# Thresholded attention and a gated two-layer block on one core: single-slot scores at the start, an earlier projection, and a new order inside a slot

## The chip, the cores and the metric

The kernel runs on one core of a Trainium2 chip. A time is device microseconds from one launch. Times before and after are medians of several runs; a profile is one more execution, with its own time. The engines are TensorE (PE, with its weight loads shown apart), VectorE (DVE), ScalarE (ACT), GpSimd (POOL) and SyncE (SP), which here only issues DMAs.

## The reference

There are 8 batches of 8 heads, with 576 rows and 64 columns each. What is computed is attention with a threshold, then two matrix products with an activation between them:

```python
scores = scale * np.matmul(q, k.transpose(0, 1, 3, 2))
thresh = np.max(scores, axis=-1, keepdims=True) - tau
scores = np.where(scores >= thresh, scores, -1000000000.0)
scores = scores - np.max(scores, axis=-1, keepdims=True)
attn = np.exp(scores)
attn = attn / (np.sum(attn, axis=-1, keepdims=True) + 1e-09)
attn_out = np.matmul(attn, v)
x = attn_out.transpose(0, 2, 1, 3).reshape(4608, 512)
h = x @ w_in                       # 512 -> 2048
g = h * np.clip(h + 3.0, 0.0, 6.0) / 6.0
out = g @ w_out                    # 2048 -> 512
```

## The kernel before

**Slots.** The work is cut into 144 slots, 18 for each batch. A slot is 128 query rows for two heads (`a` = 0, 1) against all 576 keys. Four heads form a "quad"; their q and k lie in 32-partition groups, so one slot uses two of PE's four row groups and the next slot (`i` = 1) the other two. The tiles run (quad 0: t 0, 1), (quad 1: t 0, 1), the 64 rest rows of both quads (t = 4), (quad 0: t 2, 3), (quad 1: t 2, 3), two slots for each.

**One slot's way.** Scores go from PE to PSUM in float32 (L224). DVE copies them to SBUF and takes the maximum (`sm_max`, L238). POOL makes the bias (L247). ACT masks with a Prelu (L252) and takes the exponential with its sum (L257). DVE inverts the sum (L260), POOL normalises to bf16 (`sm_norm`, L265). The result is transposed by a DMA that SP issues (L276), or, for the slots marked `on_chip`, by nine PE transposes (L282) and a DVE copy (L283). The attention product with v (L290) writes PSUM, and DVE casts it to `xT` (L298). Then the projection (`mm1`, L313 with `w_in_sb`), the activation in two steps (`mm1_relu` on ACT in odd slots and on DVE in even ones, L331 and L333; `mm1_gate` on DVE, L346), and the second projection (`mm2_part`, L313 with `w_out_sb`), whose finished token tile of 128 rows is evicted by DVE (`mm2_out`, L365) and stored.

**PSUM.** One tile holds eight banks. An even slot's scores take bank 2 (448 "own" columns) and 128 columns at the end of bank 1, an odd slot's bank 0 and 128 columns at the head of bank 1; the second head uses banks 3 to 5 in the same way. Products use banks 2 and 5 in turn (`bank()`), which are the own banks of even slots. `HB` = 6 takes the projection and the PE transposes, `OB` = 7 the second projection.

**Order.** The order of the work is written out by hand, slot by slot, in one loop; each engine runs its instructions in that order, and waits come from the data. In slot n the loop gives: the maximum of slot n+1, the inverse of slot n-1, waiting copies (PE transposes and token tiles), one projection item if n is at least `N1` = 15 and one is there, the attention products of slot n, the item's activation, a PE transpose, in odd slots two parts of the second projection, the exponentials of slot n, the masks of slot n+1, transposes of q and k (`jobs`), the normalisation of slot n-1, in even slots the scores of n+2 and n+3 together (`burst`), some filler matmuls (`warm_up`), and DMA issues (`issues`). Inside a burst a no-op on POOL stands between two groups of matmuls that share a bank.

**Items.** A projection item is 256 tokens of one batch by 256 columns of `w_in`: 8 items for each chunk of 256 tokens, and rest items for the 64 rows left of each batch. A chunk's items come free when the last of its four head pairs has had its product: for batch 0 at slots 14 and 24, then every batch at its own slots 14 and 24. Items and parts that are left after slot 143 are done after the loop.

**Loads.** SP loads q (four DMAs) and k (one) per quad into two alternating buffers; the first k goes by ACT's queue. DVE transposes them in 32x32 blocks (L104, L118). POOL loads v and the two weights, with a cast.

Of the kernel before, what the change touches and what calls it, by code (L numbers as in the profile page):

```python
# [15 lines left out]
P = 128  # L16
# [4 lines left out]
def kernel(  # L21
# [10 lines left out]
    nc = tc.nc  # L32
# [4 lines left out]
    KI = d_model // P  # L37
    NI = d_ff // P
    NSLOT = 18
    N1 = 15  # L40
    HB, OB = 6, 7
    R, T = 32, S // 32
    scale = 1.0 / math.sqrt(D)
# [24 lines left out]
    qkT = {}  # L68
# [7 lines left out]
    def at(when, n, job):  # L76
        when.setdefault(n, []).append(job)
# [4 lines left out]
    def load(quad, of, t0=0, t1=T, by=nc.sync):  # L82
        b, g = divmod(quad, 2)
        if quad not in nat:
            nat[quad] = (nat_pool.tile([P, T * D], F32, tag="nq", name="nq"),
                         nat_pool.tile([P, T * D], F32, tag="nk", name="nk"))
        dst = nat[quad][of][:, t0 * D:t1 * D]
        if of:
            src = k[b, 4 * g:4 * g + 4].rearrange("h (r t) d -> (h r) (t d)", r=R)
            by.dma_start(out=dst, in_=src[:, t0 * D:t1 * D])  # L90
            return
        for c in range(4):
            by.dma_start(out=dst[32 * c:32 * c + 32].rearrange("p (t d) -> p t d", d=D),
                         in_=q[b, 4 * g + c].rearrange("(t r) d -> r t d", r=R)[:, t0:t1])
# [7 lines left out]
    def transpose_q(quad, t0, t1):  # L102
        rows = nat[quad][0][:].rearrange("p (t j w) -> p t j w", j=2, w=32)
        nc.vector.transpose(out=qk_of(quad)[0][:].rearrange("p j (t w) -> p t j w", w=32)[:, t0:t1],  # L104
                            in_=rows[:, t0:t1])
# [3 lines left out]
    def transpose_k(quad, part):  # L109
        first, e = ((0, 5), (10, 4))[part]  # L110
        rows = nat[quad][1][:].rearrange("p (t j w) -> p j t w", j=2, w=32)
        outs = qk_of(quad)[1]
        for j in range(2):
            for_u = rows[:, j, first:first + 2 * e].rearrange("p (u e) w -> p u e w", u=2)
            base = outs[:, j, :]
            o = base[:, 64 * part:64 * part + 64].rearrange("p (u w) -> p u w", u=2)
            o = bass.AP(tensor=o.tensor, offset=o.offset, ap=[list(o.ap[0]), [32, 2], [128, e], [1, 32]])
            nc.vector.transpose(out=o, in_=for_u)  # L118
# [31 lines left out]
    load(0, 1, 0, 10, by=nc.scalar)  # L150
    load(0, 0, 0, 4)
    load(0, 1, 10, T, by=nc.scalar)
    load(0, 0, 4, T)
    load(1, 1)
    load(1, 0)

    identf = singles.tile([P, P], F32)
# [20 lines left out]
    def bank():  # L178
        nonlocal turn
        turn += 1  # L180
        return ps[:, (2, 5)[turn % 2], :]
# [7 lines left out]
    for b in range(B):  # L189
        for g, t in ((0, 0), (0, 1), (1, 0), (1, 1), (None, 4), (0, 2), (0, 3), (1, 2), (1, 3)):  # L190
            for i in range(2):
                sl = Slot()
                sl.b, sl.g, sl.t, sl.i, sl.n = b, g, t, i, len(queue)
                sl.on_chip = sl.n in (1, 3, 5, 7, 8, 9, 11)
                queue.append(sl)


# [3 lines left out]
    def score_col(n, a):  # L201
        return (512 - OWN if n % 2 else 1024 - P) + 1536 * a

    def behind(one, other):
        tc.add_manual_dep(one.ins, other.ins.name, mybir.DependencyInfo(
            mybir.DependencyClass.Sync, mybir.DependencyReason.DATA), reason="bank")

    def burst(n):
        steps = ((0, 0, P, 0), (1, 0, OWN, 0), (0, 0, P, 1), None,
                 (0, P, OWN, 0), (1, 0, OWN, 1), (0, P, OWN, 1), (1, OWN, P, 0), (1, OWN, P, 1))  # L210
        for step in steps:
            if step is None:
                relay = nc.gpsimd.nop()
                behind(relay, mm)
                continue
            i, k0, w, j = step
            sl = queue[n + i]
            for a in range(2):
                c = 32 * (2 * i + a)
                c0 = score_col(n + i, a) + k0  # L220
                for quad, rows, q0 in (((2 * sl.b + sl.g, slice(0, P), sl.t * P),) if sl.t < 4 else
                                       [(2 * sl.b + g, slice(64 * g, 64 * g + 64), 512) for g in range(2)]):
                    qT, kT = qkT[quad]
                    mm = nc.tensor.matmul(ps_flat[rows, c0:c0 + w],  # L224
                                          qT[c:c + 32, j, q0:q0 + rows.stop - rows.start],
                                          kT[c:c + 32, j, k0:k0 + w], start=(j == 0), stop=(j == 1))
                    if (i, k0) == (1, OWN):
                        behind(mm, relay)

    def sm_max(sl):  # L230
        sl.s = s_pool.tile([P, 2, S], F32, tag="s", name="s")
# [61 lines left out]
    def av_main(b, hp, chunk):  # L293
        if hp == chunk == 0:
            xT[b] = x_pool.tile([P, KI, 512], BF16, tag="xT", name="xT")
        pb = bank()[:, 0:256]
        av(pb, b, hp, pts[b, hp, chunk], slice(0, 256))
        nc.vector.tensor_copy(out=xT[b][:, hp, 256 * chunk:256 * chunk + 256], in_=pb)  # L298

# [94 lines left out]
    for b in range(B):  # L394
        n0 = b * NSLOT
        for hp in range(NPAIR):
            at(products, n0 + 8 + 2 * hp, (b, hp, 0))
            at(products, n0 + 18 + 2 * hp, (b, hp, 1))
        at(products, n0 + 16, (b, None, None))

# [14 lines left out]
    for quad in range(2, 2 * B):  # L415
        b, g = divmod(quad, 2)
        n0 = (b - 1) * NSLOT
        when = (((4, 5), (7, 8))[g] if b == 1 else ((-2, -1), (6, 7))[g])
        for n, of in zip(when, (1, 0)):
            at(issues, n0 + n, lambda quad=quad, of=of: load(quad, of))  # L420
        when = (7, 9, 11, 13) if quad == 2 else ((4, 6, 8, 10), (12, 14, 16, 18))[g]
        for n, job in zip(when, (lambda quad=quad: transpose_k(quad, 0), lambda quad=quad: transpose_k(quad, 1),
                                 lambda quad=quad: transpose_q(quad, 0, 8), lambda quad=quad: transpose_q(quad, 8, T))):
            at(jobs, n0 + n, job)
    at(jobs, 0, lambda: transpose_q(0, 4, 8))
    for n, job in ((0, lambda: transpose_k(1, 0)), (1, lambda: transpose_k(1, 1)), (2, lambda: transpose_q(1, 0, 8)),
                   (3, lambda: transpose_q(0, 8, T)), (5, lambda: transpose_q(1, 8, T))):
        at(jobs, n, job)

    def v_pieces(b, slots):  # L430
# [10 lines left out]
    v_pieces(0, (0, 0, 1, 1, 2, 2, 3, 3))  # L441
    for b in range(1, B):
        v_pieces(b, (16, 17, 18, 19, 20, 21, 22, 23) if b == 1 else [(b - 1) * NSLOT + n for n in range(8, 24, 2)])
    for i, n in enumerate((4, 6, 8, 10)):
        at(issues, n, lambda i=i: load_w_in(i))
    for i, n in enumerate((12, 13, 14, 15)):
        at(issues, n, lambda i=i: load_w_out(i))

    transpose_k(0, 0)
    transpose_k(0, 1)  # L450
    transpose_q(0, 0, 4)
    burst(0)
    sm_max(queue[0])
    for i in range(2):
        sm_mask(queue[0], i)

# [7 lines left out]
    prev = None  # L464
    pieces = bb = mt = part = 0
    waiting = []
    for n, sl in enumerate(queue):
        now = n
        late_slot = n == len(queue) - 2
        if n + 1 < len(queue):  # L470
            sm_max(queue[n + 1])
        if prev is not None:
            sm_recip(prev)
        for copy in waiting:
            copy()
        waiting = []
        item = None
        if todo1 and n >= N1:
            item, then = todo1.pop(0)
            h = mm1(item, 0 if n == len(queue) - 1 else OB if n > N1 and n % 2 == 0 and not pieces else HB)  # L480
            todo2.extend(then)
        multiply(n)
        if item:
            mm1_gate(item, h, mm1_relu(h, on_act=n % 2 == 1))
        if n > 1 and queue[n - 2].on_chip:
            waiting.append(pe_transpose(queue[n - 2]))
        second()
        for i in range(2):
            sm_exp(sl, i)
        if n + 1 < len(queue):  # L490
            for i in range(2):
                sm_mask(queue[n + 1], i)
        if part == 3:
            waiting.append(lambda tile=(bb, mt): late.extend(mm2_out(*tile, on_act=False)))
            part = 0
        for job in jobs.get(n, ()):
            job()
        if prev is not None:
            sm_norm(prev)
        if n % 2 == 0 and n + 2 < len(queue):  # L500
            burst(n + 2)
        if n < 3 or n == 6:
            warm_up(6)
        flush()
        for issue in issues.get(n, ()):
            issue()
        prev = sl

    for copy in waiting:
        copy()  # L510
    count = [1, 0 if todo2 and todo2[0][2] else 1]

    def last_tile(mt):
# [76 lines left out]
```

## Time and profile before

| | |
|---|---|
| Median of three runs | 535.21 us (533.33, 535.21, 536.99) |
| The profiled execution | 535.49 us, span 533.7 us |
| Busy: PE, DVE, ACT, POOL | 501.8, 446.7, 442.6, 281.1 us |
| Mean granted clock of PE | 0.971 |
| DMA | 80.85 MB, mean 151 GB/s |
| Last exponential of the loop starts | 491.63 us |

How to read it: times inside the profile count from the start of the span. "L238" is a line of the kernel before. The digits of the slices are busy tenths in 40 equal parts of the span, PEclk the granted clock in tenths. A DMA share over 1 means that packets overlap. In a timeline a row is a start, a length, the engine, the line, the operation, what it writes and reads, a count, and in brackets the idle time before it with what ended it. Float32 matmuls show as two instructions each, so that a burst of 16 has 32.

### The profile page before, as it was taken

To read this page: it belongs to the slowest core of one execution; us is meant where nothing else is said; L and a number is where in the kernel's file an instruction comes from. 1 tells how busy PE (TensorE), PEld (TensorE's weight loads), DVE (VectorE), ACT (ScalarE), POOL (GpSimd) and SP (SyncE) were. 2 spreads that over 40 slices of the span, in tenths; PEclk is the share of its full clock that TensorE was granted. 3 is DMA by queue.
4 is the path that set the end of the run, shared out by engine and by line. 5 is a ranking of instruction groups with operands and counts; after the bars stand their busy time and mean duration, and the time that the engine had idled before them with its cause. 6 is when DMAs were issued, how large, how long until landed. Compare 5 with 4: busy or idle time off the path is not lost.

```text
span 533.7 us, 17090 instructions
## 1 busy us (share of the span) xinstructions
PE 501.8 (94%) x6735; PEld 371.2 (70%) x6739; DVE 446.7 (84%) x1141; ACT 442.6 (83%) x949; POOL 281.1 (53%) x512
## 2 busy tenths in 40 slices
PE   6677787999999999999999999999999999999997
PEld 6454565677777777677767777677767777778465
DVE  6664776799999999999999999999999998887433
ACT  3776676899999999999999999999999999999322
POOL 1664564655565665566665655555555556555000
PEclk9987788899999999999999999999999999999999
DMA  8499699998999969898979999997999987856511
GB/s 176 57 160 218 106 128 178 174 215 136 156 161 180 184 138 185 142 174 155 194 144 183 175 157 174 160 186 127 169 169 197 159 111 143 143 111 113 120 60 41
DMA packets 229969, 80.85 MB, mean 151 GB/s; under 512 B 210688, under 2 KB 223232, under 8 KB 229888
## 3 DMA queue, kind: packets, MB, share of 16 engines
q1 hardware_dynamic: 216016, 70.12, 77.1%
q0 software_dynamic: 13440, 8.92, 14.1%
q8 instruction: 53, 0.87, 0.7%
q10 hardware_dynamic: 432, 0.72, 0.4%
q14 instruction: 28, 0.23, 0.1%
HBM read 36.70 MB, written 9.44 MB: 86 GB/s over the span
## 4 chain that ended last, share of the span: by engine, by line
PE 80%; DMA 4%; DVE 2%; issue 1%; ACT 0%; POOLq 0%; POOL 0%; DVEq 0%
PE ps L313 46%; PE ps L224 27%; PE ps L290 6%; DMA pT<-pn 4%; DVE s L238 1%; PE ps L518 1%; ACT r L331 0%; DVE g L346 0%; DVE xT L298 0%; DVE osb L521 0%; POOLq L265 0%; POOL pn L265 0%; DVE rinv L260 0%; DVEq L260 0%; DVEq L238 0%
## 5 line engine op out<-in xcount | busy, mean ns | idle before, releaser
L238 DVE TENSOR_SCALAR_CACHE_REDUCE s<-ps 128x576 f32<-128x576 f32 x288 | 205.6, 751 | 42.5 <-PE ps L224 23.5
L252 ACT ACTIVATE s<-s,bias 128x576 f32<-128x576 f32 x288 | 205.9, 763 | 25.6 <-POOL bias L247 25.4
L265 POOL TENSOR_SCALAR pn<-s,rinv 128x576 bf16<-128x576 f32 x288 | 210.9, 745 | 23.3 <-DMA pT<-pn 4.2
L224 PE MATMUL ps<-kT,qT 32*128 32x128 f32 (+3 forms) x2560 | 190.4, 438 | 21.7 <-DVE s L238 11.7
L257 ACT ACTIVATE s<-s 128x576 f32<-128x576 f32 x288 | 192.4, 671 | 0.0
L224 PEld LDWEIGHTS ps<-kT,qT 32*128 32x128 f32 (+1 forms) x2560 | 135.4, 182 | 63.3 <-DVE s L238 16.4
L313 PE MATMUL ps<-xT,w_in_sb 128*64 128x256 bf16 (+1 forms) x1936 | 133.8, 277 | 0.1
L313 PE MATMUL ps<-w_out_sb,g 128*64 128x512 bf16 (+1 forms) x1021 | 130.7, 379 | 0.2
L313 PEld LDWEIGHTS <-w_in_sb 128*64 128x64 bf16 (+1 forms) x1936 | 110.2, 110 | 28.6 <-issue 18.3
L247 POOL TENSOR_SCALAR bias<-m 128x2 f32<-128x2 f32 (+1 forms) x146 | 27.6, 189 | 175.9 <-DVE rinv L260 165.4
L346 DVE SCALAR_TENSOR_TENSOR g<-r,ps 128x512 bf16<-128x512 f32 x128 | 87.8, 687 | 10.7 <-ACT r L331 6.3
L313 PEld LDWEIGHTS <-g 128*64 128x64 bf16 (+1 forms) x1024 | 61.7, 109 | 47.9
L331 ACT ACTIVATE r<-ps,three 128x512 f32<-128x512 f32 x81 | 55.3, 686 | 40.7 <-PE ps L313 39.7
L257 ACT ACTIVATION_READ_ACCUMULATOR s<-s 128x1 f32 x288 | 54.8, 190 | 0.0
L290 PE MATMUL ps<-pT,v 128*64 128x256 bf16 x640 | 46.5, 277 | 0.8 <-DVE s L238 0.8
L290 PEld LDWEIGHTS <-v 128*64 128x64 bf16 x960 | 42.0, 112 | 3.6 <-issue 1.5
L333 DVE TENSOR_SCALAR r<-ps 128x512 f32<-128x512 f32 x63 | 42.9, 681 | 0.0
L126 POOL DMA_DIRECT2D v<-in_v_dram x64 | 36.7, 574 | 9.4 <-issue 3.5
L298 DVE CAST xT<-ps 128x256 bf16<-128x256 f32 x64 | 26.8, 419 | 11.3 <-PE ps L290 11.1
L365 DVE TENSOR_SCALAR osb<-ps 128x512 f32<-128x512 f32 x32 | 21.5, 672 | 9.1 <-PE ps L313 9.1
L118 DVE STREAM_TRANSPOSE kT<-nk 128x320 f32<-128x320 f32 (+1 forms) x64 | 26.5, 453 | 1.0 <-DMA nk<-in_k_dram 1.0
L104 DVE STREAM_TRANSPOSE qT<-nq 128x640 f32<-128x640 f32 (+2 forms) x33 | 24.8, 751 | 0.0
(31 smaller groups left out, 143.2 us busy)
## 6 DMA issues: line engine op xcount, KB each, us to landing
nk<-in_k_dram SPq DMA_DIRECT2D x15, 576.0 KB, 5.8
nq<-in_q_dram SPq DMA_DIRECT2D x60, 144.0 KB, 5.6
out_dram<-osb SPq DMA_DIRECT2D x31, 256.0 KB, 2.9
v<-in_v_dram POOLq DMA_DIRECT2D x32, 80.0 KB, 3.9
v<-in_v_dram POOLq DMA_DIRECT2D x32, 64.0 KB, 3.5
w_in_sb<-in_moe_w_in_dram POOLq DMA_DIRECT2D x4, 512.0 KB, 8.3
w_out_sb<-in_moe_w_out_dram POOLq DMA_DIRECT2D x4, 512.0 KB, 10.6
pT<-pn SPq DMA_TRANSPOSE x123, 4.0
```

The lines of the kernel that those rows point to most:

```text
L126: nc.gpsimd.dma_start(out=vsb[b % 2][32 * g:32 * g + 32].rearrange("p (hp a) c -> p a hp c", a=2)[:, a, :, c0 * D:(c0 + count) * D], in_=v ...
L224: mm = nc.tensor.matmul(ps_flat[rows, c0:c0 + w], qT[c:c + 32, j, q0:q0 + rows.stop - rows.start], kT[c:c + 32, j, k0:k0 + w], start=(j == ...
L238: nc.vector.tensor_scalar(out=sl.s[:, i, :], in0=ps_flat[:, c0:c0 + S], scalar1=1.0, scalar2=None, op0=Alu.mult, op1=Alu.max, accum_out=sl ...
L247: nc.gpsimd.tensor_scalar(out=sl.bias[:, of], in0=sl.m[:, of], scalar1=-scale, scalar2=tau, op0=Alu.mult, op1=Alu.add)
L252: nc.scalar.activation(out=s, in_=s, func=Act.Prelu, bias=sl.bias[:, i:i + 1], scale=scale, alpha=REJECT)
L257: nc.scalar.activation(out=s, in_=s, func=Act.Exp, accum_out=sl.rsum[:, i:i + 1])
L265: nc.gpsimd.tensor_scalar(out=pn[:, i, :], in0=sl.s[:, i, :], scalar1=sl.rinv[:, i:i + 1], scalar2=1.0, op0=Alu.mult, op1=Alu.mult)
L290: nc.tensor.matmul(pb[a * 64:(a + 1) * 64, :], vsb[b % 2][:, 2 * hp + a, u * D:(u + 1) * D], pT[:, block, cols], start=(c == 0), stop=(c = ...
L313: nc.tensor.matmul(out[c:c + w], lhsT[:, c:c + w], rhs, start=start, stop=stop)
L331: nc.scalar.activation(out=r, in_=hps, func=Act.Relu, bias=three[:])
L333: nc.vector.tensor_scalar(out=r, in0=hps, scalar1=3.0, scalar2=0.0, op0=Alu.add, op1=Alu.max)
L346: nc.vector.scalar_tensor_tensor(out=out, in0=r, scalar=6.0, in1=hps, op0=Alu.min, op1=Alu.mult)
```

## The change

The scores of slots 0 to 13 are made one slot at a time, by a new function, ahead of the slot's other PE work; from slot 14 on the bursts stay. The shared columns of a slot wait for a no-op on DVE, which itself waits for the scores of the slot before. The projection may begin at slot 11. In every slot the attention products now come ahead of the projection item, and its activation directly behind it. The finished token tile is evicted in the next slot behind that slot's activation, no longer ahead of it. The products of batch 0's first chunk move to slots 6, 7, 9 and 10 and use columns of bank 7 there. Loads, transposes, weight issues and the list of `on_chip` slots are set anew to fit.

```diff
-    N1 = 15
+    N1 = 11
...
+    load(1, 1, by=nc.scalar)
     load(0, 0, 4, T)
-    load(1, 1)
     load(1, 0)
...
-                sl.on_chip = sl.n in (1, 3, 5, 7, 8, 9, 11)
+                sl.on_chip = sl.n in (1, 3, 5, 6, 7, 8)
...
+    gate = [None]
+
+    def scores(n):
+        sl = queue[n]
+        quads = [(2 * sl.b + sl.g, slice(0, P), sl.t * P)] if sl.t < 4 else [
+            (2 * sl.b + g, slice(64 * g, 64 * g + 64), 512) for g in range(2)]
+        own = (P, OWN) if n % 2 == 0 else (0, OWN)
+        shared = (0, P) if n % 2 == 0 else (OWN, P)
+        for k0, w in (own, shared):
+            for j in range(2):
+                for a in range(2):
+                    c = 32 * (2 * (n % 2) + a)
+                    c0 = score_col(n, a) + k0
+                    for quad, rows, q0 in quads:
+                        qT, kT = qkT[quad]
+                        mm = nc.tensor.matmul(ps_flat[rows, c0:c0 + w],
+                                              qT[c:c + 32, j, q0:q0 + rows.stop - rows.start],
+                                              kT[c:c + 32, j, k0:k0 + w], start=(j == 0), stop=(j == 1))
+                        if (k0, w) == shared and gate[0] is not None:
+                            behind(mm, gate[0])
+        sl.last_mm = mm
+
+    def pass_on(n):
+        gate[0] = nc.vector.nop()
+        behind(gate[0], queue[n].last_mm)
...
-        pb = bank()[:, 0:256]
+        pb = ps[:, OB, P:P + 256] if now < N1 else bank()[:, 0:256]
...
-            at(products, n0 + 8 + 2 * hp, (b, hp, 0))
+            at(products, n0 + 8 + 2 * hp if b else (6, 7, 9, 10)[hp], (b, hp, 0))
...
-        when = (((4, 5), (7, 8))[g] if b == 1 else ((-2, -1), (6, 7))[g])
+        when = (((6, 7), (9, 10))[g] if b == 1 else ((-2, -1), (6, 7))[g])
...
-    at(jobs, 0, lambda: transpose_q(0, 4, 8))
-    for n, job in ((0, lambda: transpose_k(1, 0)), (1, lambda: transpose_k(1, 1)), (2, lambda: transpose_q(1, 0, 8)),
-                   (3, lambda: transpose_q(0, 8, T)), (5, lambda: transpose_q(1, 8, T))):
+    for n, job in ((0, lambda: transpose_k(1, 0)), (0, lambda: transpose_k(1, 1)), (1, lambda: transpose_q(1, 0, 8)),
+                   (2, lambda: transpose_q(0, 8, T)), (4, lambda: transpose_q(1, 8, T))):
...
-    for i, n in enumerate((4, 6, 8, 10)):
+    for i, n in enumerate((4, 5, 7, 9)):
         at(issues, n, lambda i=i: load_w_in(i))
-    for i, n in enumerate((12, 13, 14, 15)):
+    for i, n in enumerate((11, 13, 15, 17)):
         at(issues, n, lambda i=i: load_w_out(i))
...
-    burst(0)
+    scores(0)
+    pass_on(0)
     sm_max(queue[0])
+    scores(1)
+    transpose_q(0, 4, 8)
...
+        if n <= N1:
+            pass_on(n + 1)
         if n + 1 < len(queue):
             sm_max(queue[n + 1])
...
+        if n <= N1:
+            scores(n + 2)
+        multiply(n)
         item = None
         if todo1 and n >= N1:
             item, then = todo1.pop(0)
             h = mm1(item, 0 if n == len(queue) - 1 else OB if n > N1 and n % 2 == 0 and not pieces else HB)
             todo2.extend(then)
-        multiply(n)
-        if item:
             mm1_gate(item, h, mm1_relu(h, on_act=n % 2 == 1))
+        for tile in outs:
+            late.extend(mm2_out(*tile, on_act=False))
+        outs = []
...
         if part == 3:
-            waiting.append(lambda tile=(bb, mt): late.extend(mm2_out(*tile, on_act=False)))
+            outs.append((bb, mt))
             part = 0
...
-        if n % 2 == 0 and n + 2 < len(queue):
+        if n > N1 and n % 2 == 0 and n + 2 < len(queue):
             burst(n + 2)
-        if n < 3 or n == 6:
+        if n < 2:
             warm_up(6)
```

More of the change, by code (lines that the diff above doesn't have):

```diff
@@ L466 @@
     waiting = []
+    outs = []
     for n, sl in enumerate(queue):
         now = n
-        late_slot = n == len(queue) - 2
+        if n <= N1:
+            pass_on(n + 1)
         if n + 1 < len(queue):
@@ L481 @@
             todo2.extend(then)
-        multiply(n)
-        if item:
             mm1_gate(item, h, mm1_relu(h, on_act=n % 2 == 1))
+        for tile in outs:
+            late.extend(mm2_out(*tile, on_act=False))
+        outs = []
         if n > 1 and queue[n - 2].on_chip:
@@ L507 @@
         prev = sl
-    for copy in waiting:
-        copy()
+    for tile in outs:
+        late.extend(mm2_out(*tile, on_act=False))
     count = [1, 0 if todo2 and todo2[0][2] else 1]
```

## The prediction

> **What bounds the kernel now.** I read the page's slices first, then a table of 10 us stretches, then the chain that ended last, then single timelines.
>
> ```profile
> PE   6677787999999999999999999999999999999997
> PEclk9987788899999999999999999999999999999999
> DMA  8499699998999969898979999997999987856511
> ```
>
> From the eighth slice (about 93 us) TensorE (PE) is full; before that it has gaps, and its granted clock is down. The stretches show how much is to be had (columns: PE, weight load, VectorE = DVE, ScalarE = ACT and GpSimd = POOL busy, clock, DMA share, GB/s):
>
> ```profile
> 20.00:30.00 10.00, 7.03 (x88) 5.56 (x88) 5.83 (x16) 8.77 (x20) 8.21 (x15) 1.00 0.71 105
> 30.00:40.00 10.00, 7.02 (x91) 5.19 (x91) 6.61 (x20) 7.32 (x17) 5.74 (x10) 0.83 1.20 167
> ...
> 50.00:60.00 10.00, 7.61 (x64) 5.95 (x59) 6.00 (x16) 5.69 (x14) 4.48 (x8) 0.67 0.89 131
> 60.00:70.00 10.00, 8.68 (x72) 5.23 (x66) 5.57 (x16) 4.25 (x10) 5.16 (x9) 0.67 0.76 105
> 70.00:80.00 10.00, 8.17 (x152) 7.16 (x151) 9.49 (x27) 9.06 (x20) 6.77 (x13) 1.00 1.41 126
> 80.00:90.00 10.00, 7.09 (x96) 5.39 (x92) 7.36 (x18) 7.68 (x19) 4.47 (x9) 1.00 1.39 144
> ...
> 200.00:300.00 100.00, 100.00 (x1446) 73.87 (x1444) 94.73 (x243) 92.24 (x202) 58.72 (x106) 1.00 1.02 168
> ```
>
> In the first 70 us no engine is full: slots wait on one another. From 70 to 90 us it is the DMA (share 1.4). In the middle PE has 100 of 100 us, with DVE at 95% and ACT at 92%. The chain names the DMA waits of slots 19 to 23, two transposes:
>
> ```profile
> 76.89 13.75 DMA pT<-pn
> ...
> 92.47 7.17 DMA pT<-pn
> ```
>
> So a gain must come from the first 25 slots; the middle can mostly only lose.
>
> **A yardstick.** I take the start of ACT's mask (L252) of slot n as "slot n". Before: slot 2 at 17.81, 9 at 40.92, 12 at 54.69, 18 at 78.86, 24 at 102.51. Back to back, ACT needs 2.67 us a slot (slots 6 and 7: 30.60 to 33.28): two masks 1.35, two exponentials with their reads 1.32. The span runs at 2.67 x 22 = 59 us from slot 2 to 24 if nothing else holds; it takes 84.7.
>
> **Scores slot by slot, slots 0 to 13.** A burst of two slots takes 2.2 us at full clock and 4.2 at half:
>
> ```profile
> 20.32 2.23 PE L224 MATMUL ps<-kT,qT 32*128 32x128 f32 x32 [2.89 <-DVE qT L104]
> ...
> 44.01 0.74 PE L290 MATMUL ps<-pT,v 128*64 128x256 bf16 x10 [0.38 <-DVE s L238]
> 47.50 1.12 PE L282 MATMUL ps<-identb,pn 128*128 128x128 bf16 x9 [2.75 <-DVE pT L283]
> 48.54 4.22 PE L224 MATMUL ps<-kT,qT 32*128 32x128 f32 x32
> ```
>
> One slot alone is not in the trace. From below it costs half a burst, 1.1 us; from above a whole one, 2.2. I take 2.2: each slot has its own two 32-row groups, and their columns do not get fewer when the other two groups stay empty. That is up to 14 x 1.1 = 15.4 us more PE time, beside ACT's 2.67 a slot; an attention product (0.7) every other slot and a transpose (0.67) in six slots still fit. What is won: scores of n+2 need only slot n read, not a pair, so ACT need not wait every second slot (its waits for the bias sum to 25.4 us before 110 us, 7.1 of them ahead of the first slot). The added DVE no-op stands ahead of the next maximum, queued behind the previous slot's copies and transposes; behind it wait that maximum and, on PE, the shared 128 columns and all that follows. It costs nothing while DVE is on time.
>
> "TensorEngine Tiling (Array Packing)" in the Trainium skill (Theoretical Speedup) promises up to 4x for contractions of 32 rows or fewer, so it speaks against this change: two groups of four in use halve the rate. It agrees with the price from above.
>
> **Start.** The second k load goes from SP's queue to ACT's, ahead of the q rest; before, the k transposes at 12.30 waited 0.22 us for it. Slot 0 of scores ends at about 8.8 as now, slot 1 at 11.0, slot 2 at 13.2; both k transposes (1.65 us) follow slot 1's maximum and end near 14.1; slot 2's maximum ends at 15.5, its bias allows the mask at 15.9. That is 1.9 us early. POOL (bias 0.2, two normalisations 1.47, two v issues 1.11 = 2.8 a slot) holds slots 3 to 5 a little: slot 6 near 27.0 (before 30.60).
>
> **Loads moved.** Quad 2's k is issued after slot 6 instead of 4, and is still transposed at 7. On SP it stands behind slot 4's transpose, whose normalisation ends near 28.2; with 2.1 us of issue (the row at 32.15) and 5 to 8.4 us to landing it arrives at about 36. DVE wants it at about 30.5. So DVE stops some 5 us, with it the no-op, and slot 9 comes at about 39.2 (36 + 0.9 transpose + 1.4 maximum + bias): 1.7 ahead only. If the load lands early this gives 4 us back. After this gap PE is half speed for one or two stretches of 3.4 us; the single-slot scores then take up to 4.2, and slot 12 is at about 49.5 instead of 47.2. Gain so far 5.2.
>
> The clock here: with 1.67 us busy between 42.7 and 46.1 the next 3.4 us were granted 0.51, though no gap exceeded 2.75 us. The Trainium skill, "TensorE: Matmul & The Clock Gate" (Part 1), wants at least one idle window of 3.4 us for that; the row is stricter. By the rule only the 5 us gap would cost clock and slot 12 would be the same.
>
> **Projection from slot 11.** Items run at 11 to 18, then 24 on (before 15 to 22, 25 on): the second chunk's products still end at 24. Before, slots 16 to 20 with an item each take 12.16 / 4 = 3.04 us. I take 3.2 with the quad transposes: slot 18 at 68.7, gain 10.2. Slots 19 to 23 have no item, so 2.67 each would give slot 24 at 84.7, gain 17.8. Here the DMA is late next: the stretches' shares times their lengths sum to 107 us up to slot 24, about 36 of them done by 39 us. The rest, 71, at the highest share seen (1.41) takes 50 us, at 1.3 it takes 55: slot 24 at 90 to 94. The loads of w_out are spread over 11, 13, 15, 17, and slots 9 and 11 go to the DMA in place of 6, so the sum is nearly unchanged. I take 92.5: **gain 10**.
>
> **The middle, slots 24 to 143.** Two effects meet.
>
> ```profile
> 304.17 0.71 PE L290 MATMUL ps<-pT,v 128*64 128x256 bf16 x10
> ...
> 304.53 0.67 DVE L365 TENSOR_SCALAR osb<-ps 128x512 f32<-128x512 f32 x1
> ...
> 304.81 2.55 PE L224 MATMUL ps<-kT,qT 32*128 32x128 f32 x32
> 305.12 0.41 DVE L298 CAST xT<-ps 128x256 bf16<-128x256 f32 x1
> ```
>
> The burst at 304.81 must wait for the cast at 305.12 to free its bank, and that stands behind the token tile's eviction. Pairs of slots with an eviction take 6.70 us (304.81 to 311.51), without 6.43 (to 317.94). With the product first and the eviction behind the gate, all can take 6.43: 30 x 0.27 = 8 us at most, nothing at least if DVE (95%) is the limit; with the eviction late, DVE still has the same work. Against it: the item is now taken after the products of its slot, so the first item of 14 groups uses an xT whose last quarter is just being cast. The product would end at 303.9; three quarters of the first column block take 0.33; the cast ends at 304.86, and with 0.19 to the release PE stands 0.6 to 0.8 us. 14 x 0.6 = 8.4, up to 12; nothing if DVE runs ahead. I take 7.4 won and 8.4 lost: **1 lost**, bounds 8 won to 12 lost.
>
> **Tail.** One item less (8 of the 64 matmuls that take 7.40 us: 0.93) and two parts of the second projection less (8 of 72 in 15.70: 1.74), since both run one and two slots earlier: **2.7 won**, all on PE, which sets the end there.
>
> **Sum.** The profiled execution: 535.49 (span 533.7 and 1.8 around it; 0.28 above the median 535.21). 535.5 - 10 + 1 - 2.7 = 523.8, so **524 us**.
>
> **Rivals.**
> 1. The DMA does not bind: slot 24 at 84.7, 17.8 won; 535.5 - 17.8 + 1 - 2.7 = 516. For it: a share of 1.41 is an average of latencies, not a ceiling, and w_out is spread. Against: the two waits of 13.75 and 7.17 fall exactly there. Chance 0.20.
> 2. The transposes bind as now: loads wanted in less time, the same late landings, and cold clock after the k wait at single-slot prices. Gain to slot 24 only 1 to 3: 535.5 - 2 + 1 - 2.7 = 532. For it: the DMA is at nine tenths from 27 us nearly throughout. Chance 0.18.
> 3. Slower: the fresh xT. If every one of the 14 group starts costs 0.86 (12 us) and DVE gives nothing back for the later eviction, the middle loses 12; it decides as soon as the first 24 slots win under 9.3. With 3 won there: 535.5 - 3 + 12 - 2.7 = 542. For it: PE has no idle time in the middle to absorb a wait. Against: DVE had 5% left. Chance 0.17.
> That the change does not do what it says is excluded by the order of the instructions: 14 slots of single scores, first projection right after the fourteenth.
>
> My forecast has 0.45. The range, 514 to 541, takes in the unbound DMA with a little won in the middle, and most of rival 3. Within 1% (5.4 us, about what a measurement of this kernel can tell from no change: three runs span 3.7) lies rival 2. Faster 0.64, same 0.19, slower 0.17.
>
> **What would show it.** Slot masks at about 15.9, 39, 49.5, 69, 92; a DVE wait on nk near 31 to 36; score groups of 2.2 us for one slot; DMA share of 1.3 or more from 40 to 90 us; in the middle 6.4 us a pair and PE waiting 0.6 for xT's cast at 14 places; the last exponential about 9 us earlier, the tail 2.7 shorter. I am wrong if single-slot scores cost clearly more than a burst, if the k wait is absent, or if the middle's 3.25 us a slot moves by more than 0.1.

## The result, and the profile after

The changed kernel takes **551.38 us** (median of four, 551.14 to 551.56) against 535.06 us (533.33 to 536.99) of the kernel before: the ratio is 1.0304, with an interval of 1.0268 to 1.0340. It is 3% slower; 524 us was forecast, and the range ended at 541. The profiled execution took 551.56 us, span 549.8. (Some of the kernels tried below have executions several us apart, in step with their clock; for these the single executions are given.)

Cut at the yardstick, the profiled executions give:

| | to slot 24 | slot 24 to 143 | behind it | span |
|---|---|---|---|---|
| before | 102.51 | 386.56 | 44.63 | 533.7 |
| after | 120.54 | 387.27 | 41.99 | 549.8 |
| difference | +18.0 | +0.7 | -2.6 | +16.1 |
| forecast | -10 | +1 | -2.7 | -11.7 |

The last two parts came as forecast, the middle by luck, as its two terms show below. The whole miss is in the first 24 slots: 28 us.

The slices of the changed kernel's page:

```profile
PE   8999987789899989999999999999999999999997
PEclk8555579979999999999999999999999999999999
DMA  8259498999989997999699989998898966865431
```

PE is busier than before in the first five slices, and its clock is at 5 for four slices. Before, the lowest digit was 7. The stretches (columns as in the prediction):

```profile
10.00:20.00 10.00, 10.00 (x52) 6.83 (x50) 6.84 (x19) 6.22 (x13) 2.81 (x8) 0.50 0.37 47
20.00:30.00 10.00, 10.00 (x44) 5.62 (x43) 3.37 (x9) 4.89 (x12) 4.65 (x9) 0.50 0.38 59
30.00:40.00 10.00, 10.00 (x52) 6.38 (x49) 4.86 (x15) 5.99 (x13) 5.67 (x11) 0.50 0.61 95
...
60.00:70.00 10.00, 10.00 (x59) 5.97 (x55) 3.17 (x9) 3.50 (x8) 3.19 (x6) 0.50 0.47 71
70.00:80.00 10.00, 7.89 (x78) 6.35 (x80) 7.32 (x18) 5.69 (x13) 4.03 (x7) 0.84 0.94 152
```

From 10 to 70 us PE has no idle time at all, and every 10 us were granted 0.50. ACT, which was to set the pace here, is busy for a third to two thirds of the time. The chain that ended last agrees:

```profile
2.14 5.39 DMA nq<-in_q_dram
8.16 9.22 PE ps L246 x44
...
46.75 4.05 PE ps L246 x32
...
58.30 4.14 PE ps L246 x16
...
71.13 2.15 PE ps L246 x16
...
98.15 14.58 DMA pT<-pn
```

A slot's scores (L246, the new function) take 4.1 us up to slot 12 and 2.15 in slot 13, at 71 us. The same matmuls cost twice as much for 61.4 us on end, and the chain runs through them. The first row is the first q: it landed 5.39 us after its issue.

### The profile page after: what moved, and what is told of

The parts are those of the page before. It is cut to its first block, busy times and chain, and to the rows that moved or that the text cites. A ratio compares the mean times of both kernels' runs of the same rounds, so it can differ in the third digit from the quotient of the medians.

```text
span 549.8 us, 17176 instructions
## 1 busy us (share of the span) xinstructions
PE 520.5 (95%) x6734; PEld 374.3 (68%) x6734; DVE 445.8 (81%) x1142; ACT 441.6 (80%) x947; POOL 280.8 (51%) x512
## 4 chain that ended last, share of the span: by engine, by line
PE 77%; DVE 14%; DMA 4%; issue 3%; ACT 2%; SPq 0%; DVEq 0%
PE ps L340 36%; PE ps L224 23%; PE ps L246 9%; DVE s L265 6%; PE ps L317 6%; DMA pT<-pn 3%; DVE g L373 2%; ACT r L358 2%; DVE xT L325 1%; PE ps L309 1%; DMA nq<-in_q_dram 1%; DVE go L373 1%; DVE r L360 1%; DVE osb L392 1%; PE ps L553 1%
## 5 line engine op out<-in xcount | busy, mean ns | idle before, releaser
L224 PE MATMUL ps<-kT,qT 32*128 32x128 f32 (+3 forms) x2304 | 152.6, 421 | 6.2 <-DVE s L265 6.1
L224 PEld LDWEIGHTS ps<-kT,qT 32*128 32x128 f32 (+1 forms) x2304 | 113.6, 178 | 47.0 <-DVE s L265 9.6
L340 PE MATMUL ps<-xT,w_in_sb 128*64 128x256 bf16 (+1 forms) x1944 | 135.4, 274 | 10.3 <-DVE xT L325 10.2
L340 PEld LDWEIGHTS <-w_in_sb 128*64 128x64 bf16 (+1 forms) x1944 | 106.2, 109 | 21.7 <-issue 14.4
L360 DVE TENSOR_SCALAR r<-ps 128x512 f32<-128x512 f32 x64 | 44.0, 688 | 12.0 <-PE ps L340 11.6
L246 PE MATMUL ps<-kT,qT 32*128 32x448 f32 (+3 forms) x256 | 51.6, 671 | 1.5 <-DVE qT L104 1.5
L317 PE MATMUL ps<-pT,v 128*64 128x256 bf16 x640 | 48.2, 284 | 2.6 <-DVE s L265 1.9
L246 PEld LDWEIGHTS ps<-kT,qT 32*128 32x128 f32 (+1 forms) x256 | 28.3, 284 | 24.1 <-issue 18.5
L126 POOL DMA_DIRECT2D v<-in_v_dram x64 | 36.8, 574 | 10.3 <-PE ps L224 5.8
```

What stands on the lines that cost most here:

```text
L126: nc.gpsimd.dma_start(out=vsb[b % 2][32 * g:32 * g + 32].rearrange("p (hp a) c -> p a hp c", a=2)[:, a, :, c0 * D:(c0 + count) * D], in_=v ...
L224: mm = nc.tensor.matmul(ps_flat[rows, c0:c0 + w], qT[c:c + 32, j, q0:q0 + rows.stop - rows.start], kT[c:c + 32, j, k0:k0 + w], start=(j == ...
L246: mm = nc.tensor.matmul(ps_flat[rows, c0:c0 + w], qT[c:c + 32, j, q0:q0 + rows.stop - rows.start], kT[c:c + 32, j, k0:k0 + w], start=(j == ...
L317: nc.tensor.matmul(pb[a * 64:(a + 1) * 64, :], vsb[b % 2][:, 2 * hp + a, u * D:(u + 1) * D], pT[:, block, cols], start=(c == 0), stop=(c = ...
L340: nc.tensor.matmul(out[c:c + w], lhsT[:, c:c + w], rhs, start=start, stop=stop)
L360: nc.vector.tensor_scalar(out=r, in0=hps, scalar1=3.0, scalar2=0.0, op0=Alu.add, op1=Alu.max)
```

## The experiments

Three theories run through the expectations. **A, the clock:** PE loses its full clock early, and work on two of four row groups, even without a gap, doesn't get it back (in its strict form, doesn't hold it either). **B, the start:** the second k load on ACT's queue delays the first q, and this wait lets the clock fall. **C:** the moved loads and the earlier projection cost, not the clock. Later runs test the late load of quad 2's k and the middle, and put the parts together.

The parts of each profiled execution in us, with the sum of the spells at half clock:

| kernel | to slot 24 | slot 24 to 143 | behind it | half clock |
|---|---|---|---|---|
| before | 102.5 | 386.6 | 44.6 | 31 |
| after | 120.5 | 387.3 | 42.0 | 73 |
| e1_k_on_sp | 119.4 | 387.3 | 42.0 | 72 |
| e2_bursts | 109.7 | 387.6 | 42.0 | 24 |
| e3_filler | 115.1 | 387.3 | 42.0 | 38 |
| e4_single_only | 120.9 | 386.5 | 44.6 | 58 |
| e5_item_first | 120.4 | 374.2 | 45.9 | 75 |
| e7_clock_and_loads | 99.5 | 387.3 | 42.0 | 17 |
| e8_order_item_first | 101.8 | 374.9 | 46.0 | 27 |
| e9_all | 95.7 | 374.2 | 45.9 | 10 |
| e10_late_k | 101.6 | 387.5 | 44.7 | 31 |
| e11_four_groups | 113.1 | 387.3 | 42.0 | 38 |
| e14_late_k_warm | 108.0 | 387.3 | 42.0 | 31 |

The early part and the middle are independent: no edit of the one moved the other by more than 1 us.

### The single-slot scores alone

e4_single_only is the kernel before, with nothing but the scores of the change (bursts from slot 14 on; the new functions are those of the change):

```diff
-    burst(0)
+    scores(0)
+    pass_on(0)
     sm_max(queue[0])
+    scores(1)
...
+        if n <= 11:
+            pass_on(n + 1)
         if n + 1 < len(queue):
             sm_max(queue[n + 1])
...
-        if n % 2 == 0 and n + 2 < len(queue):
+        if n <= 11:
+            scores(n + 2)
+        elif n % 2 == 0 and n + 2 < len(queue):
             burst(n + 2)
```

> The kernel before with one part of the change alone: scores of slots 0 to 13 one slot at a time with the no-op on DVE, at the place of the burst; loads, projection from slot 15 and the order in a slot as before. Theory A: half clock through most of the first 60 us, 543 to 555 us. Theory B: q is on time, so the clock holds for a while and falls with the first gap; 535 to 545 us. Theory C: 533 to 537 us, as before.

Measured: 554.84 us, ratio 1.0395 (1.0342 to 1.0448). Two of its stretches:

```profile
20.00:30.00 10.00, 9.08 (x40) 5.79 (x39) 2.94 (x9) 4.20 (x11) 3.96 (x8) 0.50 0.40 59
...
70.00:80.00 10.00, 9.31 (x56) 6.65 (x59) 4.57 (x11) 4.96 (x11) 3.30 (x6) 0.50 0.16 30
```

This one part costs 20 us, with the loads and the fillers of the kernel before: PE nine tenths busy, clock 0.50. So neither the late k nor the k load on ACT's queue is needed for the loss.

e2_bursts does the opposite: the changed kernel with bursts throughout.

```diff
-    scores(0)
-    pass_on(0)
+    burst(0)
     sm_max(queue[0])
-    scores(1)
...
-        if n <= N1:
-            pass_on(n + 1)
...
-        if n <= N1:
-            scores(n + 2)
...
-        if n > N1 and n % 2 == 0 and n + 2 < len(queue):
+        if n % 2 == 0 and n + 2 < len(queue):
             burst(n + 2)
-        if n < 2:
+        if n < 3 or n == 6:
             warm_up(6)
```

> The changed kernel with bursts of two slots from slot 0 on, and the filler matmuls of the kernel before; all else as changed (loads, projection from 11, new order in a slot). Theories A and B: the clock is up in most of the first 70 us as before the change, the loss of 18 us is gone: 526 to 536 us. Theory C: 545 to 552 us.

Measured: 542.65 us, ratio 1.0139 (1.0069 to 1.0209). The half clock falls from 73 to 24 us, but slot 24 still comes 7.2 us later than in the kernel before. Slot 2 is already 4.5 us later (22.35), as the first q landed 6.70 us after its issue. What PE and DVE wait for between 38 and 75 us (waiting operation and what it waits for: us in total, times, longest):

```profile
PE ps L309 <- DVE pT L310: 9.1, 1, 9.1
...
DVE kT L118 <- DMA nk<-in_k_dram: 6.3, 1, 6.3
```

The late k stops DVE for 6.3 us, a copy stands behind it, and PE waits 9.1 for that copy. So this isn't a clean undo: with bursts the late k is exposed. In the changed kernel it is hidden: DVE never waits for it there, and from slot 6 to slot 9 it takes 15.4 us even so, against 10.3 in the kernel before.

### What holds the clock down

e1_k_on_sp puts the second k load back on SP's queue:

```diff
-    load(1, 1, by=nc.scalar)
     load(0, 0, 4, T)
+    load(1, 1)
     load(1, 0)
```

> The changed kernel with one part undone: the second k load goes back to SP's queue behind the rest of the first q. Theory A (two row groups do not give PE enough activity to lift its clock, nor to hold it): q comes on time, scores start at 6.6 instead of 8.2 us, yet the clock falls within the first 20 us and stays at half until the projection starts; 547 to 551 us. Theory B (the 1.5 us of waiting for q lets the clock fall, and only cold it cannot rise): the clock stays at 1.0 past 40 us, slot 14's mask comes near 55 to 62 us instead of 84.6, total 524 to 532 us. Theory C (the moved loads and the earlier projection are what costs, not the clock): no more than 1 us from 551.

Measured: four executions of 550.47, 543.41, 549.20 and 537.36 us, with mean clocks of 0.935, 0.950, 0.935 and 0.965. Slot 2 comes at 16.4 instead of 19.34, so the start is mended in the profiled one, the first. Its clock:

```profile
10.00:20.00 10.00, 9.77 (x52) 5.97 (x49) 6.20 (x20) 8.21 (x18) 4.75 (x11) 0.69 0.54 63
20.00:30.00 10.00, 10.00 (x49) 6.51 (x49) 4.93 (x14) 5.33 (x11) 5.40 (x10) 0.50 0.32 51
...
60.00:70.00 10.00, 10.00 (x56) 5.94 (x52) 5.67 (x16) 1.44 (x2) 2.54 (x5) 0.50 0.74 125
```

It fell at 13.7 us instead of 9.5, and stayed down for the same 61.4 us. So the late q isn't needed for the clock to go. But by their mean clocks the four executions spent some 71, 54, 71 and 37 us at half clock, the four of the changed kernel 69 to 73 each: with q on time the spell is at times much shorter, and what decides that isn't shown.

e3_filler adds 18 filler matmuls, which use the whole array, behind slot 2's scores:

```diff
-            warm_up(6)
+            warm_up(24 if n == 0 else 6)
```

> The changed kernel with 24 instead of 6 full-array filler matmuls behind the scores of slot 2 (about 5.9 us at half clock, 2.9 at full). Theory A in its strong form (two row groups neither lift nor hold the clock): full clock for one or two stretches of 3.4 us, then half again: 550 to 555 us. Theory B (they hold what full-array work has lifted): full clock from about 20 us on, slot 14 some 15 us earlier, 533 to 541 us. Theory C: 553 to 556 us, the fillers come on top.

Measured: 547.87 us (543.07 to 550.38), ratio 1.0245 (1.0172 to 1.0317).

```profile
20.00:30.00 10.00, 10.00 (x72) 7.66 (x72) 4.96 (x14) 5.45 (x13) 4.71 (x10) 0.83 0.41 61
30.00:40.00 10.00, 9.24 (x80) 5.20 (x80) 7.70 (x23) 9.52 (x22) 8.92 (x17) 1.00 0.62 93
...
50.00:60.00 10.00, 9.31 (x52) 6.18 (x52) 5.17 (x15) 5.54 (x12) 4.04 (x7) 0.53 0.92 171
60.00:70.00 10.00, 10.00 (x49) 5.83 (x49) 4.72 (x14) 1.44 (x2) 3.97 (x7) 0.50 0.66 107
```

The fillers raised the clock at 23.3 us, and the single-slot scores, with the products and PE transposes among them, then held it for 27.3 us. At 50.6 it fell, after DVE had waited 4.0 us for quad 2's k, and didn't come back until 74.5. So the strict form of the clock theory, that such scores can't keep the clock, is wrong: they can hold it, but after a gap they didn't raise it for 24 us.

e11_four_groups fills the two idle row groups in slots 0 to 6: beside each score matmul runs a companion of the same shape on the other groups, into spare banks. It only adds work.

```diff
+                        if n <= 6:
+                            i = 32 * (2 * ((n + 1) % 2) + a)
+                            mm = nc.tensor.matmul(ps[:, (OB, HB)[a], 0:w], qT[i:i + 32, j, q0:q0 + P],
+                                                  kT[i:i + 32, j, k0:k0 + w], start=(j == 0), stop=(j == 1))
+                            if gate[0] is not None:
+                                behind(mm, gate[0])
```

> The changed kernel; for slots 0 to 6 each single-slot score matmul gets a companion of the same shape on one of the two idle row groups, into banks 6 and 7, which nothing reads. The companions wait for the no-op, which may cost 0.2 to 0.5 us a slot. Theory A (a half-empty array is not active enough to lift the clock): with four groups in use the clock comes back to 1.0 within two or three stretches, between 13 and 35 us, and slots 3 to 7 then take 2.7 to 3.2 us each. Rival (it is not the groups; float32 scores, or the order of waits, keep the clock down): half clock until 70 us as in the changed kernel, each slot 0 to 0.5 us longer, 551 to 555 us in total.

Measured: 544.17 us, ratio 1.0178 (1.0145 to 1.0212): 7 us less than the changed kernel with twice the score matmuls in seven slots.

```profile
10.00:20.00 10.00, 10.00 (x138) 7.19 (x136) 8.17 (x25) 7.75 (x17) 4.47 (x11) 1.00 0.40 48
20.00:30.00 10.00, 9.04 (x103) 6.21 (x97) 5.27 (x15) 8.78 (x20) 8.13 (x15) 0.85 0.73 107
30.00:40.00 10.00, 9.80 (x118) 5.53 (x116) 5.97 (x18) 7.02 (x15) 5.77 (x11) 0.98 0.80 129
40.00:50.00 10.00, 5.50 (x29) 3.48 (x29) 4.40 (x13) 3.83 (x10) 2.32 (x4) 0.70 1.15 234
50.00:60.00 10.00, 10.00 (x53) 5.81 (x51) 3.92 (x13) 4.34 (x10) 4.04 (x7) 0.50 0.37 56
```

This decides between theory A and its rival. Between 10 and 20 us PE is 100% busy in both kernels, with the same loads and the same late q. With two row groups in use the clock is 0.50, with four it is 1.00; and where it fell at 27 us it was back within 4 us. (The companions fill the idle groups and so double the matmuls and weight loads at work; no run parts the two.) The companions end with slot 6. Then comes the wait for k (DVE 4.8 us), the clock falls at 44, and with the single-slot scores that follow PE is full, or nearly, at 0.50 until 74.8.

### The late loads

e10_late_k gives the kernel before the late loads of quads 2 and 3, and nothing else:

```diff
-        when = (((4, 5), (7, 8))[g] if b == 1 else ((-2, -1), (6, 7))[g])
+        when = (((6, 7), (9, 10))[g] if b == 1 else ((-2, -1), (6, 7))[g])
```

> The kernel before with one part of the change alone: quads 2 and 3 are loaded after slots 6, 7, 9, 10 instead of 4, 5, 7, 8. If the late k stops DVE: a DVE wait on nk of 3 to 7 us near 40 us, PE idle behind it, total 537 to 544. If the transposes are late anyway: 533 to 537.

Measured: 537.57 us, ratio 1.0016 (0.998 to 1.0052): no difference. In its profiled execution slot 24 comes at 101.6, 0.9 earlier, and DVE waits 0.7 us for the late k. The cost expected of it isn't there.

e7_clock_and_loads mends all three suspects in the changed kernel: k on SP (the edit of e1), fillers (that of e3), early loads.

```diff
-    load(1, 1, by=nc.scalar)
     load(0, 0, 4, T)
+    load(1, 1)
...
-        when = (((6, 7), (9, 10))[g] if b == 1 else ((-2, -1), (6, 7))[g])
+        when = (((4, 5), (7, 8))[g] if b == 1 else ((-2, -1), (6, 7))[g])
...
-            warm_up(6)
+            warm_up(24 if n == 0 else 6)
```

> The changed kernel with 24 filler matmuls behind the scores of slot 2, the second k load back on SP's queue, and the k and q loads of quads 2 and 3 issued after slots 4, 5, 7, 8 as before the change. If two things cost (the clock, which single-slot scores hold but cannot lift, and the late k, whose wait lets it fall): full clock from about 20 us on, no DVE wait on nk, 2.7 to 3.0 us a slot up to slot 10, slot 14 at 55 to 64 us, total 518 to 530 us. If single-slot scores cannot hold the clock either: half clock again by 45 us, total 540 to 552. If the late k does not matter: as with the fillers alone, 543 to 548.

Measured: 530.61, 541.10, 528.76 and 543.04 us, at mean clocks of 0.984, 0.959, 0.990 and 0.959. The profiled one is the first: slot 24 at 99.5, 21 us earlier than in the changed kernel and 3 earlier than before the change. The median of the four, 535.86, is that of the kernel before, run beside it (535.95).

e14_late_k_warm is e7 without its early loads, so that the late k stands alone against a clock that is up:

```diff
-        when = (((4, 5), (7, 8))[g] if b == 1 else ((-2, -1), (6, 7))[g])
+        when = (((6, 7), (9, 10))[g] if b == 1 else ((-2, -1), (6, 7))[g])
```

> The changed kernel with 24 fillers behind the scores of slot 2 and the second k load on SP's queue, so that the clock is up at the start, but quads 2 and 3 loaded late as in the change. It differs from the run with clock and loads both mended by the late k alone. If the late k costs once the scores run at full clock: a DVE wait on nk of 4 to 7 us near 35 to 45 us, PE idle over a whole stretch of 3.4 us and half clock after it, slot 14 at 74 to 82 us instead of 65, total 538 to 546 in all executions. If the wait is hidden: 528 to 531 in the executions that hold the clock.

Measured: 538.66 us, ratio 1.0088 (1.006 to 1.0117). A wait between 25 and 75 us, in the form used for e2:

```profile
DVE kT L118 <- DMA nk<-in_k_dram: 4.0, 1, 4.0
```

and a stretch behind it:

```profile
50.00:60.00 10.00, 10.00 (x58) 6.18 (x58) 5.59 (x16) 1.44 (x2) 1.87 (x5) 0.50 0.67 116
```

Slot 24 is at 108.0, 8.5 us behind the profiled execution of e7. So a late load that is free in the kernel before costs 8.5 here: 4.0 are the wait, and the half clock after it, from 43.0 to 66.9 us, goes with the rest. That holds against the executions of e7 that keep their clock (528.8 and 530.6); its other two are as long as these without a late load.

### The middle

e5_item_first is the changed kernel, with the projection item chosen before the products of its slot, as it was, but still issued behind them:

```diff
-        multiply(n)
         item = None
         if todo1 and n >= N1:
             item, then = todo1.pop(0)
+        multiply(n)
+        if item:
             h = mm1(item, 0 if n == len(queue) - 1 else OB if n > N1 and n % 2 == 0 and not pieces else HB)
```

> The changed kernel, but the projection item of a slot is chosen before the slot's products are made, so that an item never uses an xT quarter cast in its own slot; one item more stays for after the loop. If the fresh xT is what costs in the middle (waits of 0.7 to 0.9 us at 14 places): slots 24 to 143 take 377 to 381 us instead of 387.3, the tail is 0.9 to 2.6 longer, total 6 to 10 us less than the changed kernel. If DVE sets the pace of the middle: 387 us as now, total 1 to 3 us more. The first 24 slots stay as they are in both.

Measured: 545.49 us, ratio 1.0166 (1.0113 to 1.022), 5.9 less than the changed kernel, and 9.3 less by the profiled executions. In the profiled executions the middle drops from 387.3 to 374.2, so the fresh `xT` cost 13.1 us there; the part behind the last slot, which now has one item more, is 3.9 longer.

e8_order_item_first brings this order to the kernel before, with its bursts and loads as they were:

```diff
             item, then = todo1.pop(0)
-            h = mm1(item, 0 if n == len(queue) - 1 else OB if n > N1 and n % 2 == 0 and not pieces else HB)
-            todo2.extend(then)
         multiply(n)
         if item:
+            h = mm1(item, 0 if n == len(queue) - 1 else OB if n > N1 and n % 2 == 0 and not pieces else HB)
+            todo2.extend(then)
             mm1_gate(item, h, mm1_relu(h, on_act=n % 2 == 1))
+        for tile in outs:
+            late.extend(mm2_out(*tile, on_act=False))
+        outs = []
...
-            waiting.append(lambda tile=(bb, mt): late.extend(mm2_out(*tile, on_act=False)))
+            outs.append((bb, mt))
```

> The kernel before with only the new order in a slot (products, then projection and its activation, then the eviction of the token tile), and the item chosen before the products so that no fresh xT is used; bursts, loads, projection from slot 15 as before. If the order itself frees PE: 6.3 us a pair in the middle, 377 to 381 us from slot 24 to 143 instead of 386.6, total 525 to 530. If DVE sets the pace: 533 to 537.

Measured: **525.09 us** (524.34 to 526.16), ratio 0.9794 (0.9761 to 0.9827). It beats both kernels. The middle is 11.7 us shorter than before, and the part behind it 1.3 longer; its pairs of slots are 6.30 us apart, with an eviction or without, in PE's timeline:

```profile
304.87 2.23 PE L224 MATMUL ps<-kT,qT 32*128 32x128 f32 x32
...
311.17 2.23 PE L224 MATMUL ps<-kT,qT 32*128 32x128 f32 x32
...
317.47 2.23 PE L224 MATMUL ps<-kT,qT 32*128 32x128 f32 x32
```

e9_all puts the edits of e7 and e5 together:

```diff
+    load(1, 1)
...
+        when = (((4, 5), (7, 8))[g] if b == 1 else ((-2, -1), (6, 7))[g])
...
+            item, then = todo1.pop(0)
+        multiply(n)
+        if item:
...
+            warm_up(24 if n == 0 else 6)
```

> The changed kernel with the fillers, the loads as before the change and the item chosen before the products: the two mends of the start and the one of the middle together. If they add: a middle of 375 us, the first 24 slots at 100 us where the clock holds and some 12 us later where it falls, total 516 to 521 us in the one case and 528 to 533 in the other. If the middle's gain needs the old start: 526 to 531 and 538 to 543.

Measured: 517.61, 530.69, 530.92 and 517.74 us, at mean clocks of 0.990, 0.963, 0.963 and 0.993. The gains add up: in the profiled one, the first, slot 24 comes at 95.7 and the middle takes 374.2. But half of its executions are 13 us longer, and the median of the four, 524.2, is within 1 us of e8's.

### What the half clock costs in the better order

e12_order_fillers adds six fillers to every early slot of e8; e13_fillers_bank7 lets them write to bank 7 instead of 6; e16_some_fillers keeps bank 7 and fewer slots. All three spoil the output (in bank 6 a filler writes over a PE transpose before its copy; what it is in bank 7 stays open), so they only price the clock. Each edit is shown against the run before it.

```diff
-        if n < 3 or n == 6:
+        if n < N1:
             warm_up(6)
```

> The kernel before with the new order in a slot and the item chosen first, and six filler matmuls behind the burst or the products of each slot below 15 (not only slots 0, 1, 2 and 6). If the half-clock stretches of the old start cost time: full clock up to 60 us, 3 to 8 us less than with the order alone, 517 to 522. If the slots wait for each other and not for PE: 524 to 527.

```diff
-            nc.tensor.transpose(ps[:, HB, 0:P], identf[:], identf[:])
+            nc.tensor.transpose(ps[:, OB, 0:P], identf[:], identf[:])
```

> The kernel before with the new order in a slot, the item chosen before the products, and six full-array fillers at the end of every slot below 15, written into bank 7, which nothing else uses until slot 16. If the half-clock stretches of the old start are worth what the fillers in bank 6 showed: 517 to 521 us, the four executions within 2 us of each other. If the wait of the fillers for bank 6 shaped that result: 522 to 527.

```diff
-        if n < N1:
+        if n < 7 or n in (8, 10, 12):
             warm_up(6)
```

> The kernel before with the new order in a slot, the item chosen before the products, and six fillers into bank 7 at the end of slots 0 to 6, 8, 10 and 12, where a score burst, a PE transpose or nothing of half-column form follows on PE. If the old start loses time to half clock: 518 to 523 us against 525 with the order alone. If the slots wait for each other: 524 to 527.

Measured: 519.19, 518.45 and 518.61 us, ratios 0.9717 (0.9683 to 0.9752), 0.9713 (0.9677 to 0.975) and 0.9699 (0.965 to 0.9748). The half clock falls from 27 us to 10, 14 and 10, and slot 24 comes at 96.0, 95.5 and 94.5 instead of 101.8. So 14 to 17 us at half clock, where they are scattered among bursts, are worth 6 to 7.

## Why the prediction was wrong

**Scores slot by slot: the price was right, its clock wasn't.** One slot takes 2.15 us at 71 us, as priced from above. But "up to 14 x 1.1 = 15.4 us more PE time" was reckoned at full clock throughout. At half clock a slot's scores cost 4.1 to 4.2; all fourteen kept PE busy for 51.6 us instead of 14 x 2.2 = 30.8, and with their transposes and products PE was full from 10 to 70 us. Instead of ACT's 2.67 a slot, PE set the pace, at 5.7 a slot on average from slot 2 to 12: slot 12 came at 76.22 instead of 49.5. The rows of before couldn't show this: they had half clock only after gaps, and score work on two row groups alone not at all. Its effect on the clock was an operation that the trace didn't show, and should have been bounded from both sides like the price.

**Loads moved: the failed step, the price of the clock.** "After this gap PE is half speed for one or two stretches of 3.4 us" is the only place where the sum has a clock, and it put 2.3 us on it (slot 12 at 49.5 instead of 47.2). The half clock lasted 61.4 us, 18 such stretches, and had begun at 9.5 us, long before quad 2's k was issued (42.45). The lateness itself was sized well (some 5 us forecast; 4.0, 4.8 and 6.3 in e14, e11 and e2), but in the changed kernel nothing waits for it: the sign "if the k wait is absent" was met. The rule weighed here was the wrong one too: the question wasn't how the clock is lost but how it is won back. The Trainium skill, "TensorE: Matmul & The Clock Gate" (Part 1), gives full clock after one window of about 3.4 us of sustained busy time; here PE was 100% busy for 60 us at 0.50, and e11 shows that filling the idle row groups made the difference. The measurement decides.

**Start: one transfer too cheap.** The second k load on ACT's queue was taken to be free. The first q then landed after 5.39 us, and slot 2 came at 19.34. With the load back on SP (e1, e14, e7) slot 2 is at 16.1 to 16.4, where 15.9 was forecast.

**Projection from slot 11 and the DMA: about right once the rest is mended.** From slot 12 to 24 e7 takes 42.5 us (57.02 to 99.54); 43.0 was forecast (49.5 to 92.5), and the kernel before takes 47.8. The waits for the DMA transposes that I expected to bind are there, 14.58 us of the chain in the changed kernel. Two terms of that sum were misread: the stretches of before add up to 105 and not 107 to slot 24, and to 31 and not 36 by 39 us; the 74 left would give slot 24 at 91.5 to 96, which still holds the 92.5. Of the whole gain of 10 to slot 24, e9 reaches 6.8 (95.7), in an execution with 10 us of half clock.

So the 18.0 us divide, by profiled executions: mending the clock and the start brings slot 24 from 120.5 to 108.0 (e14), the early k on top of it to 99.5 (e7). The first 12.5 aren't split further by a run: in its profiled execution e1 moved the start without moving the clock and got 1.1; e3 moved the clock without the start and got 5.5, though its first q landed later still (7.31 us).

**The middle: right as a sum by luck, wrong in both terms.** The lines of the changed kernel's timeline that answer to those of before:

```profile
302.64 0.71 PE L317 MATMUL ps<-pT,v 128*64 128x256 bf16 x10
...
303.87 0.40 DVE L325 CAST xT<-ps 128x256 bf16<-128x256 f32 x1
304.15 2.23 PE L224 MATMUL ps<-kT,qT 32*128 32x128 f32 x32
...
305.60 0.68 DVE L392 TENSOR_SCALAR osb<-ps 128x512 f32<-128x512 f32 x1
```

The cast now stands ahead of the eviction, the burst follows it at once, and between 200 and 330 us the pairs without a fresh `xT` take 6.27 to 6.39 us, most of them 6.30; I had expected them to stop at the 6.43 of the pairs without eviction. So the order wins 12 (e5, e8: 386.6 to 374.2 and 374.9) instead of 7.4. And the fresh `xT` costs 13.1 instead of 8.4, more than the bound of 12. Its wait is in the list of 200 to 480 us, 0.76 each, which I had put at 0.6 to 0.8:

```profile
PE ps L340 <- DVE xT L325: 7.6, 10, 0.9
```

Fourteen of these are 10.6. The other 2.5 arise in the same places: exactly 14 pairs of slots of the changed kernel's middle take 7.11 to 7.41 us, 0.80 to 1.13 more than the same pairs in e5, and these differences add up to 13.1. Net 0.7 lost, against 1: two terms, each some 4.6 us too small, cancel.

**Tail:** 2.64 won, 2.7 forecast.

**Rivals.** Rival 3 was to lose through the fresh `xT`; its 12 us were there, and the order gave 12 back. Of the rivals only the second had the clock, and only behind the k wait, as a small term. A range for "half clock for all fourteen slots" would have been 14 x 2 = 28 us on PE, enough to reach the measured time; that it equals the miss is chance, since the scores took 21 us more than priced and the late q came on top.

## What to carry to other kernels

When an edit makes matmuls use fewer row groups, price it at half clock as well as at full, and look at the granted clock of every 10 us and not only at the busy time: a PE that is 100% busy can still be running at half speed. A late load may cost nothing in one order of work and 8.5 us in another, where the work that follows the gap doesn't bring the clock back. A change with several parts is worth taking apart even when its sum is bad: one part here, the order in the slot with the item chosen early, wins 2% by itself.

## What the runs showed of the hardware that was not expected

- Float32 matmuls, most of them on two of four row groups, kept PE 100% busy from 10 to 70 us at a granted clock of 0.50. With companions on the other two groups the clock was 1.00 from 10 to 20 us (e11).
- The same work can hold a clock that is up: 27.3 us in e3, and in e9 all fourteen slots' scores, from 6.5 to 50.2 us, ran at full clock.
- And the clock isn't always lost for good. It rose five times in the midst of single-slot scores: in e3 at 23.3, e4 at 31.4 and 48.5, e7 at 41.2, and in the changed kernel at 71.0 us. Each time the 3.4 us before held 2.2 to 2.8 us of work on all four row groups (fillers, PE transposes and products; in e4 1.54 us of fillers and 1.17 of transposes, which overlap a little). Six other stretches with 2.2 to 2.4 us of it, in e1, e3, e14 and the changed kernel, were followed by half clock all the same, and so was, among single-slot scores without companions, every one with less. How much is needed to keep the clock up, no run here settles.
- Executions of one kernel differ by its early clock: 528.8 and 530.6 against 541.1 and 543.0 us in e7, 517.6 and 517.7 against 530.7 and 530.9 in e9. e8, with bursts, stayed within 524.3 to 526.2.
- With a second k load on ACT's queue the first q, on SP's, landed 5.39 us after its issue and the scores started at 8.16 us (10.07 in e3, where it took 7.31); with that load behind q on SP they started at 7.09 (e1) and 6.71 (e7).
